# One branch per half of an expert's job, the narrow half in line, with counts and positions read later

## The chip, the cores and the metric

The kernel runs on one NeuronCore of one Trainium2 chip. Its time is the device time of one execution in microseconds (us). Five engines take part: TensorE (PE, the matrix engine), VectorE (DVE), ScalarE (ACT), GpSimd (POOL) and SyncE (SP), which here only issues DMAs. Each engine runs its own instruction stream; semaphores order them against each other, and when the program branches on a value, every engine takes the branch in its own stream.

## The reference

Three layers in float32, one after another, on 1152 tokens of width 512:

```python
attn: phi(x) = [exp(p - max|p|), exp(-(p - max|p|))], p = x @ w_phi
      out = phi(q) @ (phi(k)^T v) / (phi(q) @ sum(phi(k)) + 1e-6)       # 2 x 8 heads, 576 tokens, 64 wide
moe:  expert_idx = argmax(x @ w_gate); each expert keeps its first 288 tokens
      y = relu(x_e @ w1[e]) @ w2[e]; out[token] = gate * y               # 8 experts, F = 1024
moe2: P = exp(logits - max), 8 rounds of row and column normalisation
      out = sum over e of P[:, e] * (relu(x @ w1[e]) @ w2[e])            # 8 experts, all tokens
```

## The kernel before

Every float32 product is made of three matmuls: each operand is split into a high part (H) and a rest (L), and H*H, L*H and H*L are added up in PSUM (`three`, lines 198 to 200). The high part of a weight tile is a copy on ACT (`split`, L155), the rest a subtraction on DVE or POOL (L158). The same pair for data that leave PSUM is L193 on ACT and L194 on DVE (`split2`).

The attention fills the first 143 us of the span. The first mixture layer (149 to 336 us) is eight jobs, one for each expert. A job is wide if its expert has more than 128 tokens: the 288 token columns are the moving operand (`job_wide`). Otherwise it is narrow, with 128 tokens (`job_narrow`). With these inputs jobs 0, 1 and 4 are wide and 2, 3, 5, 6 and 7 narrow. Which one runs is decided on the chip: `tc.If(counts[j] > P)` holds the wide job, `Else` the narrow one, so a narrow job jumps over the wide one, and a wide job jumps over the narrow one at its end. On PE a wide job is some 200 rows of the program and a narrow one some 110.

A job has two halves. The first multiplies the tokens x1 by the expert's w1 and keeps the ReLU as h1; the second multiplies h1 by w2 and writes the tokens' result to x2H and x2L. In the second half the next job's tokens are transposed (`win_T`, L668, into x1H and x1L) and the next expert's w1 tiles are split (w0H, w0L: the name counts from 0), and as each split ends the DMA of the tile after that is issued on SP (L144 for w1 in two pieces of 256 KB, L147 for w2). A narrow job transposes its hidden result with `turn_h` (L721), makes its second product in two pieces of 256 columns, evicts them as yn0 and yn1 (L749), transposes these (L759) and splits the result into x2H and x2L.

PSUM tiles come from a ring of five banks, pb0 to pb4, counted by `ring["n"]` while the program is written. The two branches of a job start from one value of the counter; after both the wide job's value stands. When a bank is used again, its first writer waits for the last reader of the use before. Before the first job stand the reads of the counts and of `kept_r` into registers on every engine, the first tokens' transposes, 12 copies each that zero x2H (POOL) and x2L (DVE), and `positions()` (12 small operations on DVE and nine scatters to `tk` on POOL), with the load of `tokc` on SP.

The second mixture layer (336 us to the end) takes a fast branch: 32 units, all but the first of seven products each (`unit`, `prod` L1001), with the products by w2 of the unit before (`second`) between them. Unit 0 is plain (`first_plain`) and prepares the mixed operands (`mix`, on DVE, POOL and ACT); of its eight second products four follow it at once and four stand in unit 1. `sink_at` gives the places of the normalisation steps.

Of the kernel before, what the change touches and what calls it, by code (L numbers as in the profile page):

```python
# [13 lines left out]
AF = mybir.ActivationFunctionType  # L14
# [6 lines left out]
def kernel(  # L21
# [15 lines left out]
    nc = tc.nc  # L37
    B, H, S, D = q.shape
    N, DM = out.shape
    E, _, F = moe_w1.shape  # L40
    P = 128
# [83 lines left out]
    class Weights:  # L125
# [8 lines left out]
        def load(self, i, which, p):  # L134
            if i >= len(self.seq):
                return
            e = self.seq[i][2]
            src = self.seq[i][which]
            t = self.raw[which, p]
            if which == 0:  # L140
                a = src[e].rearrange("(c p) (h q f) -> q p c h f", p=P, h=2, f=P)[p]
                t = t.rearrange("p a (b h f) -> p (a b) h f", h=2, f=P)
                for h in range(2):
                    nc.sync.dma_start(out=t[:, :, h, :], in_=a[:, :, h, :])  # L144
            else:
                a = src[e].rearrange("(h q p) d -> q p h d", p=P, h=2)[p]
                nc.sync.dma_start(out=t, in_=a)  # L147

        def split(self, i, which, p, eng=None, copy=None):
# [493 lines left out]
    with ExitStack() as mctx:  # L643
# [32 lines left out]
        def job_wide(j, off_r):  # L676
            i, w = jobs[j]
            hint(j)
            for kk, f in enumerate(FO):
                ps = bank(W)  # L680
                for c in range(NC):
                    three(ps, wt.w1(f, c), x1[c], c, NC)
                evict_split(h1H[:, kk, :], h1L[:, kk, :], ps, relu=True)
                if i > 0 and kk < 4 and w == 0:
                    wt.split(i, 1, kk)
            pg = prep(0)
            for d in range(NC):
                ps = bank(W)
                for kk, f in enumerate(FO):
                    wH, wL = wt.w2(f)  # L690
                    three(ps, (wH[:, d * P:(d + 1) * P], wL[:, d * P:(d + 1) * P]),
                          (h1H[:, kk, :], h1L[:, kk, :]), kk, NFC)
                evict_split(x2H[:, d, ds(off_r, W)], x2L[:, d, ds(off_r, W)], ps)
                for c in ((0, 1), (2,), (3,), ())[d]:
                    win_T(j + 1, c)
                if d == 2:
                    win_load(j + 2)
                if w == NW - 1:
                    if i + 1 < E:
                        wt.split(i + 1, 0, d)  # L700
                    else:
                        next(pg)

        def job_narrow(j, off_r):
            i, w = jobs[j]
            hint(j)
            pool = {(1, 3), (0, 1), (0, 3)}

            pg = prep(0)

            def split(i, which, p):
                if i == E:
                    next(pg)
                else:
                    wt.split(i, which, p, nc.gpsimd if (which, p) in pool else None)

            def turn_h(g):
                ps = bank4()
                for f in range(4):
                    o = f % 2 * P  # L720
                    nc.tensor.transpose(ps[:, f, :], hn[2 * g + f // 2][:, o:o + P], ident)  # L721
                split2(h1H[:, 4 * g:4 * g + 4, 0:P], h1L[:, 4 * g:4 * g + 4, 0:P], ps)

            if i > 0:
                split(i, 1, 0)
            for p in range(4):
                ps = bank(256)
                for c in range(NC):
                    three(ps, (x1[c][0][:, 0:P], x1[c][1][:, 0:P]), wt.w1p(p, c), c, NC)
                nc.scalar.activation(out=hn[p], in_=ps, func=AF.Relu)  # L730
                if i > 0 and p < 3:
                    split(i, 1, p + 1)
                if p == 1:
                    ring["n"] += 1
                if p == 2:
                    turn_h(0)
            win_T(j + 1, 0)
            win_T(j + 1, 1)
            turn_h(1)
            ring["n"] += 1  # L740
            split(i + 1, 0, 0)
            split(i + 1, 0, 1)
            for g in range(2):
                ps = bank(256)
                for kk, f in enumerate(FO):
                    wH, wL = wt.w2(f)
                    n = slice(g * 256, (g + 1) * 256)
                    three(ps, (h1H[:, kk, 0:P], h1L[:, kk, 0:P]), (wH[:, n], wL[:, n]), kk, NFC)
                nc.scalar.activation(out=yn[g], in_=ps, func=AF.Copy)  # L749
                if g == 0:  # L750
                    win_T(j + 1, 2)
                    split(i + 1, 0, 2)
            win_T(j + 1, 3)
            win_load(j + 2)
            ring["n"] += 1
            ps = bank4()
            for c in range(NC):
                o = c % 2 * P
                nc.tensor.transpose(ps[:, c, :], yn[c // 2][:, o:o + P], ident)  # L759
            split(i + 1, 0, 3)  # L760
            split2(x2H[:, :, ds(off_r, P)], x2L[:, :, ds(off_r, P)], ps)
# [33 lines left out]
                src[0:1, j:j + 1], min_val=0, max_val=N, skip_runtime_bounds_check_because=why,  # L795
                **({"engines": engines} if engines else {}))

        kept_r = scalar(kept_i, 0)
        counts = [scalar(cnt_i, j) for j in range(E)] if NW == 1 else None
        for c in range(NC):  # L800
            win_T(0, c)
        win_load(1)
        for t, eng in ((x2H, nc.gpsimd), (x2L, nc.vector)):
            for c in range(NC):
                for o in range(0, N, 512):
                    n = min(512, N - o)
                    eng.tensor_copy(t[:, c, o:o + n], zero[:, 0:n])
        positions()
        nc.sync.dma_start(out=tokc, in_=tk.rearrange("(t p) o -> p t o", p=P))
        for j in range(len(jobs)):  # L810
            off_r = scalar(off_i, j, DYN)
            if NW > 1:
                job_wide(j, off_r)
                continue
            n0 = ring["n"]
            with tc.If(counts[j] > P) as cmp:
                job_wide(j, off_r)
            n1, ring["n"] = ring["n"], n0
            with cmp.Else():
                job_narrow(j, off_r)  # L820
            ring["n"] = n1

    skp = ctx.enter_context(tc.tile_pool(name="skp", bufs=1))
    gms = skp.tile([P, 96], F32, name="gms")
# [117 lines left out]
    def moe2_fast(fp):  # L942
# [88 lines left out]
                put(t)  # L1031

        pending = [sink_start, sink_max, sink_exp, sink_row] + [lambda it=it: sink_col(it) for it in range(8)]
        sink_at = ((1, 3), (1, 6), (2, 0), (2, 1), (2, 3), (2, 5), (2, 7), (3, 1), (3, 3), (3, 5), (3, 7), (4, 1))

        def relu_split(dst, src):
            hi, lo = dst
# [4 lines left out]
        def first_plain():  # L1042
# [5 lines left out]
            for i in range(4):  # L1048
# [12 lines left out]
                if i == 0:  # L1061
                    for c in range(NC):
                        gate2(c)
                    sink_logits()
            next(ms[1])
            next(ms[0])
            wt.load(E + 1, 0, 1)
            for t in range(4):
                second(0, t)
                if t < 2:  # L1070
                    next(ms[1])
            return [slots[4], slots[5]]

# [55 lines left out]

        spare = first_plain()  # L1130
        for g in range(1, 4 * E):
            spare = unit(g, spare, list(range(4 if g == 1 else 0, 8)))
        for t in range(8):
            second(4 * E - 1, t)

# [37 lines left out]
```

## Time and profile before

| what | value |
|---|---|
| median of 3 runs | 1014.09 us (1012.7 to 1018.23) |
| profiled execution | 1013.54 us, its span 1011.8 us |
| attention / first layer / second layer, from the first matmul of each | to 149.13 / 149.13 to 336.01 / 336.01 to 1011.8 us |
| PE busy | 960.1 us, 95% of the span |
| mean granted TensorE clock | 0.98 |
| starts of jobs 0 to 7 on PE | 149.13, 180.19, 211.59, 233.72, 249.43, 281.91, 297.77, 319.15 us |

PE is nearly always busy in the second layer; its idle time lies in the first 370 us, above all between jobs. So the page's shares say little, and the timeline around each job says most: a row there is a start, a duration, the engine, the line, the operation with its tiles, and in brackets the idle time of the engine ahead of it with what ended it. "issue" means that the profile shows nothing that the engine waited for.

### The profile page before, as it was taken

How to read it: one execution, taken by the hardware profiler on the slowest of the kernel's cores; microseconds unless marked ns; L12 is line 12 of the kernel's file. 1: busy time of each engine (PE TensorE's matmuls, PEld its weight loads, DVE VectorE, ACT ScalarE, POOL GpSimd, SP SyncE). 2: the span in 40 equal slices, each digit the busy share in tenths (PEclk: the TensorE clock that was granted, in tenths of full speed). 3: DMA queues.
4: the chain of work that ended last, by engine and by line, in shares of the span. 5: the costliest groups of instructions: out<-in, count | busy, mean ns of one | idle time of the engine just before them, and what ended most of it. 6: DMA issues, size and time to landing. Idle time of an engine off the chain costs nothing.

```text
span 1011.8 us, 14034 instructions
## 1 busy us (share of the span) xinstructions
PE 960.1 (95%) x5329; PEld 836.6 (83%) x5329; DVE 607.2 (60%) x1074; ACT 371.6 (37%) x621; POOL 415.4 (41%) x398
## 2 busy tenths in 40 slices
PE   8999969987987989999999999999999999999997
PEld 8999968977986767888888888888888888888886
DVE  4667765655554668856655565556555655565555
ACT  4456522556565343242232223222322232222320
POOL 2244234013023653554345434553355335533533
PEclk9999989988989999999999999999999999999999
DMA  7697121668778311122112211221122111200002
GB/s 124 142 276 248 62 87 28 194 195 226 208 203 240 94 50 42 53 63 63 41 43 63 63 42 42 63 63 41 42 62 64 43 42 48 76 23 1 1 1 84
DMA packets 123291, 89.66 MB, mean 89 GB/s; under 512 B 34529, under 2 KB 101345, under 8 KB 123201
## 3 DMA queue, kind: packets, MB, share of 16 engines
q1 hardware_dynamic: 120240, 83.65, 29.4%
q0 software_dynamic: 1728, 4.73, 1.2%
q8 instruction: 54, 0.88, 0.4%
q14 instruction: 37, 0.30, 0.1%
q10 hardware_dynamic: 1232, 0.10, 0.1%
HBM read 79.01 MB, written 9.45 MB: 87 GB/s over the span
## 4 chain that ended last, share of the span: by engine, by line
PE 79%; issue 8%; DVE 7%; ACT 2%; DMA 2%; POOL 2%; ACTq 0%; POOLq 0%; DVEq 0%; SPq 0%
PE pb L1001 27%; PE pb L198 14%; PE pb L199 14%; PE pb L200 14%; PE pb L310 3%; PE pb L445 3%; PE pb L428 1%; DMA raw<-in_moe_w_dram 1%; PE pb L668 1%; DVE hidL L1039 1%; POOL out_dram L177 1%; DVE snap L978 1%; PE pb L254 1%; DMA wg<-in_moe_w_gate_dram 1%; DVE w1L L158 0%
## 5 line engine op out<-in xcount | busy, mean ns | idle before, releaser
L1029 DVE SCALAR_TENSOR_TENSOR oc<-pb,Pm,oc 128x512 f32<-128x512 f32 x224 | 167.2, 749 | 93.8 <-PE pb L200 92.7
L955 POOL TENSOR_TENSOR w1L<-raw,w1H 128x1024 fp32r<-128x1024 f32 x32 | 77.0, 2408 | 336.1 <-ACT w1H L954 336.1
L198 PE MATMUL pb<-w1H,hidH 128*128 128x512 f32 x512 | 199.7, 390 | 3.8 <-ACT oc L1023 2.3
L200 PE MATMUL pb<-w1H,hidL 128*128 128x512 f32 x512 | 199.3, 389 | 0.0
L199 PE MATMUL pb<-w1L,hidH 128*128 128x512 f32 x512 | 199.3, 389 | 0.0
L1038 ACT ACTIVATE hidH<-snap 128x512 fp32r<-128x512 f32 x93 | 58.8, 632 | 241.6 <-DVE snap L1116 112.1
L1001 PE MATMUL pb<-x2H,w0H 128*128 128x512 f32 x310 | 121.6, 392 | 0.0
L1001 PE MATMUL pb<-x2L,w0H 128*128 128x512 f32 x310 | 120.7, 389 | 0.0
L1001 PE MATMUL pb<-x2H,w0L 128*128 128x512 f32 x310 | 120.6, 389 | 0.0
L198 PEld LDWEIGHTS pb<-w1H,hidH 128*128 128x128 f32 x512 | 96.2, 188 | 24.7 <-ACT oc L1023 2.8
L200 PEld LDWEIGHTS pb<-w1H,hidL 128*128 128x128 f32 x512 | 96.2, 188 | 20.0
L199 PEld LDWEIGHTS pb<-w1L,hidH 128*128 128x128 f32 x512 | 96.2, 188 | 20.0
L1039 DVE SCALAR_TENSOR_TENSOR hidL<-snap,hidH 128x512 fp32r<-128x512 f32 x93 | 64.6, 695 | 64.9 <-ACT hidH L1038 64.9
L640 POOL TENSOR_TENSOR w0L<-stmp,w0H 128x1024 fp32r<-128x1024 f32 x31 | 75.1, 2422 | 0.3 <-ACT w0H L637 0.3
L1001 PEld LDWEIGHTS pb<-x2H,w0L 128*128 128x128 f32 x310 | 58.2, 188 | 12.2
L1001 PEld LDWEIGHTS pb<-x2H,w0H 128*128 128x128 f32 x310 | 58.2, 188 | 11.9
L1001 PEld LDWEIGHTS pb<-x2L,w0H 128*128 128x128 f32 x310 | 58.2, 188 | 11.8
L158 POOL TENSOR_TENSOR w1L<-raw,w1H 128x1024 fp32r<-128x1024 f32 x9 | 21.7, 2409 | 109.6 <-ACT w1H L155 109.2
L635 POOL TENSOR_TENSOR w0L<-raw,w0H 128x512 fp32r<-128x512 f32 x64 | 65.3, 1044 | 0.2 <-ACT w0H L624 0.2
L1038 ACT ACTIVATE hidH<-pb 128x512 fp32r<-128x512 f32 x35 | 20.9, 596 | 88.9 <-PE pb L1001 88.9
L1001 PE MATMUL pb<-w1H,w0H 128*128 128x512 f32 x124 | 48.8, 394 | 0.0
L1001 PE MATMUL pb<-w1L,w0H 128*128 128x512 f32 x124 | 48.7, 393 | 0.0
(246 smaller groups left out, 1967.0 us busy)
## 6 DMA issues: line engine op xcount, KB each, us to landing
raw<-in_moe_w_dram SPq DMA_DIRECT2D x128, 256.0 KB, 3.6
raw<-in_moe_w_dram SPq DMA_DIRECT2D x64, 512.0 KB, 3.9
xe<-zero SPq DMA_DIRECT2D x18, 256.0 KB, 4.1
xw<-xe SPq DMA_DIRECT2D x7, 576.0 KB, 7.5
v<-in_v_dram SPq DMA_DIRECT2D x8, 256.0 KB, 5.0
q<-in_q_dram SPq DMA_DIRECT2D x8, 256.0 KB, 5.7
k<-in_k_dram SPq DMA_DIRECT2D x7, 256.0 KB, 4.8
xw<-xe SPq DMA_DIRECT2D x4, 144.0 KB, 2.7
```

What stands on the lines that cost most here:

```text
L198: nc.tensor.matmul(ps, lhsT=aH, rhs=bH, start=i == 0, stop=False)
L199: nc.tensor.matmul(ps, lhsT=aH, rhs=bL, start=False, stop=False)
L200: nc.tensor.matmul(ps, lhsT=aL, rhs=bH, start=False, stop=i == n - 1)
L310: nc.tensor.matmul(kvps[b][g // 4][:, g % 4, 0:MW], lhsT=kp[:, h, half, :], rhs=vv[:, h * VW:h * VW + MW], start=first and g % 4 == 0, sto ...
L445: nc.tensor.matmul(ps[:, h, 0:MW], lhsT=qt[:, g, :], rhs=kv[b][:, g * KW:g * KW + MW], start=half == 0, stop=half == 1,)
L635: tt(out=aL[:, o, :], in0=w, in1=aH[:, o, :].bitcast(F32), op=ALU.subtract)
L640: tt(out=sL, in0=wide(tmp), in1=sH.bitcast(F32), op=ALU.subtract)
L955: nc.gpsimd.tensor_tensor(out=lo, in0=r, in1=hi.bitcast(F32), op=ALU.subtract)
L1001: nc.tensor.matmul(o, lhsT=a[x][:, c, :], rhs=b[c][y], start=first and c == 0 and m == 0, stop=c == 1 and m == 2, skip_group_check=True)
L1029: nc.vector.scalar_tensor_tensor(out=o, in0=ps, scalar=gate, in1=o, op0=ALU.mult, op1=ALU.add)
L1038: nc.scalar.activation(out=hi, in_=src, func=AF.Relu)
L1039: nc.vector.scalar_tensor_tensor(out=lo, in0=src, scalar=0.0, in1=hi.bitcast(F32), op0=ALU.max, op1=ALU.subtract)
```

## The change

It has five parts.

1. Each job becomes two `tc.If`, one for each half, through generators with a `yield` between the halves. The test is turned round: the narrow half stands in line, and the wide half is the `Else`. All ring counts go on from the wide half, as before.
2. In a narrow job the second product is one of 512 columns in one bank. Its two evictions stand together behind it, and the split of w0 tile 2, which stood between the two pieces, stands behind them.
3. The counts are read behind the first transposes; `kept_r`, `positions()` and the load of `tokc` are put ahead of job 1; x2L is zeroed on POOL.
4. A w1 tile is loaded by one DMA of 512 KB with 1 KB pieces in place of two DMAs with 512 B pieces, by another assignment of the hidden columns to tiles; w2 follows that order.
5. In the second layer all eight `second(0, t)` stand ahead of unit 1; the stages of the operand mix stand between the last of them, and the normalisation steps get other places.

```diff
-                a = src[e].rearrange("(c p) (h q f) -> q p c h f", p=P, h=2, f=P)[p]
-                t = t.rearrange("p a (b h f) -> p (a b) h f", h=2, f=P)
-                for h in range(2):
-                    nc.sync.dma_start(out=t[:, :, h, :], in_=a[:, :, h, :])
+                a = src[e].rearrange("(c p) (q n) -> q p c n", p=P, n=2 * P)[p]
+                nc.sync.dma_start(out=t.rearrange("p a (b n) -> p (a b) n", n=2 * P), in_=a)
...
-                a = src[e].rearrange("(h q p) d -> q p h d", p=P, h=2)[p]
+                a = src[e].rearrange("(q h p) d -> q p h d", p=P, h=2)[p]
...
+            yield
             pg = prep(0)
...
+            yield
             win_T(j + 1, 0)
             win_T(j + 1, 1)
             turn_h(1)
...
+            ps = bank(512)
+            for kk, f in enumerate(FO):
+                three(ps, (h1H[:, kk, 0:P], h1L[:, kk, 0:P]), wt.w2(f), kk, NFC)
+                if kk == 3:
+                    win_T(j + 1, 2)
             for g in range(2):
-                ps = bank(256)
-                for kk, f in enumerate(FO):
-                    wH, wL = wt.w2(f)
-                    n = slice(g * 256, (g + 1) * 256)
-                    three(ps, (h1H[:, kk, 0:P], h1L[:, kk, 0:P]), (wH[:, n], wL[:, n]), kk, NFC)
-                nc.scalar.activation(out=yn[g], in_=ps, func=AF.Copy)
-                if g == 0:
-                    win_T(j + 1, 2)
-                    split(i + 1, 0, 2)
+                nc.scalar.activation(out=yn[g], in_=ps[:, g * 256:(g + 1) * 256], func=AF.Copy)
+            split(i + 1, 0, 2)
             win_T(j + 1, 3)
...
-        kept_r = scalar(kept_i, 0)
-        counts = [scalar(cnt_i, j) for j in range(E)] if NW == 1 else None
         for c in range(NC):
             win_T(0, c)
         win_load(1)
-        for t, eng in ((x2H, nc.gpsimd), (x2L, nc.vector)):
+        counts = [scalar(cnt_i, j) for j in range(E)] if NW == 1 else None
+        for t, eng in ((x2H, nc.gpsimd), (x2L, nc.gpsimd)):
...
-        positions()
-        nc.sync.dma_start(out=tokc, in_=tk.rearrange("(t p) o -> p t o", p=P))
         for j in range(len(jobs)):
+            if j == 1:
+                positions()
+                nc.sync.dma_start(out=tokc, in_=tk.rearrange("(t p) o -> p t o", p=P))
+                kept_r = scalar(kept_i, 0)
             off_r = scalar(off_i, j, DYN)
...
-            n0 = ring["n"]
-            with tc.If(counts[j] > P) as cmp:
-                job_wide(j, off_r)
-            n1, ring["n"] = ring["n"], n0
-            with cmp.Else():
-                job_narrow(j, off_r)
-            ring["n"] = n1
+            narrow_job = job_narrow(j, off_r)
+            for _ in range(2):
+                n0 = ring["n"]
+                with tc.If(counts[j] < P + 1) as cmp:
+                    next(narrow_job, None)
+                ring["n"] = n0
+                with cmp.Else():
+                    next(wide_job, None)
...
-            next(ms[1])
-            next(ms[0])
             wt.load(E + 1, 0, 1)
-            for t in range(4):
+            for t in range(8):
                 second(0, t)
-                if t < 2:
+                if t == 4:
+                    next(ms[0])
+                if t >= 4 and t < 7:
                     next(ms[1])
...
-            spare = unit(g, spare, list(range(4 if g == 1 else 0, 8)))
+            spare = unit(g, spare, list(range(8 if g == 1 else 0, 8)))
```

On PE, before, this is the end of narrow job 2 and the start of the wide version of job 3, which the narrow job 3 jumps over. The names with a number are tiles; pb3_129 is a PSUM bank.

```order
L668 MATMUL pb1_127<-ident_72,xw_1881 128x96 x3
L759 MATMUL pb3_129<-ident_72,yn0_1896 128x128 [waits Activation_49]
L759 MATMUL pb3_129<-ident_72,yn0_1896 128x128
L759 MATMUL pb3_129<-ident_72,yn1_1897 128x128 [waits Activation_49]
L759 MATMUL pb3_129<-ident_72,yn1_1897 128x128
L816 UNCONDITIONAL_BRANCH
L816 COMPARE_AND_BRANCH
L198 MATMUL pb4_130<-x1H0_1882,w0H0_142 128x288 [waits DVE_49,Activation_49]
```

The last transposes go to bank pb3, and job 3 begins in pb4. Now the same end of job 2, and behind it, on PE, the start of narrow job 3 (some 100 rows of the wide half lie between the two fences):

```order
L666 MATMUL pb2_128<-ident_72,xw_1873 128x96 x3
L757 MATMUL pb4_130<-ident_72,yn0_1888 128x128 [waits Activation_49]
L757 MATMUL pb4_130<-ident_72,yn0_1888 128x128
L757 MATMUL pb4_130<-ident_72,yn1_1889 128x128 [waits Activation_49]
L757 MATMUL pb4_130<-ident_72,yn1_1889 128x128
L819 UNCONDITIONAL_BRANCH
```

```order
L819 UNCONDITIONAL_BRANCH
L819 COMPARE_AND_BRANCH
L196 MATMUL pb4_130<-w0H0_142,x1H0_1874 128x256 [waits DVE_49,Activation_49]
L197 MATMUL pb4_130<-w0L0_143,x1H0_1874 128x256
L198 MATMUL pb4_130<-w0H0_142,x1L0_1875 128x256
```

The last transposes of job 2 and the first product of job 3 now share bank pb4, so the wait on DVE in the first row of job 3 is now for the reader of those transposes, the split into x2L.

On ACT, before, this is the second half of narrow job 2:

```order
L749 ACTIVATE yn0_1896<-pb3_129 128x256 [waits PE_49]
L193 ACTIVATE x1H2_1886<-pb4_130 128x288 [waits DVE_49,PE_49]
L155 ACTIVATE w0H2_146<-raw02_136 128x1024 [waits DMAHW6_49,DMAHW7_49,DMAHW5_49,Activation_49]
L749 ACTIVATE yn1_1897<-pb0_126 128x256 [waits DVE_49,PE_49]
L193 ACTIVATE x1H3_1888<-pb1_127 128x288 [waits DVE_49,PE_49]
L155 ACTIVATE w0H3_148<-raw03_137 128x1024 [waits DMAHW0_49,DMAHW1_49,Activation_49,Pool_49]
L193 ISA
L193 ACTIVATE x2H_1876<-pb3_129 128x4x128 [waits PE_49]
```

And now, on ACT in the same place:

```order
L191 ACTIVATE x1H2_1878<-pb1_127 128x288 [waits DVE_49,PE_49]
L749 ACTIVATE yn0_1888<-pb0_126 128x256 [waits PE_49]
L749 ACTIVATE yn1_1889<-pb0_126 128x256
L153 ACTIVATE w0H2_146<-raw02_136 128x1024 [waits DMAHW7_49,DMAHW0_49]
L191 ACTIVATE x1H3_1880<-pb2_128 128x288 [waits DVE_49,PE_49]
L153 ACTIVATE w0H3_148<-raw03_137 128x1024 [waits DMAHW1_49,Pool_49]
L191 ISA
L191 ACTIVATE x2H_1868<-pb4_130 128x4x128 [waits PE_49]
```

Behind the last matmul of the second product there are now two evictions, two weight copies and two splits, where there were one, one and two. (Lines of the changed file are two lower here: its L191 is L193 of before.)

## Rows read from the trace of the kernel before

**Rows 1.** The page: PE's busy time, share of the span, instructions.
```profile
PE   960.1 (95%) x5329; PEld 836.6 (83%) x5329; DVE 607.2 (60%) x1074; ACT 371.6 (37%) x621; POOL 415.4 (41%) x398
```

**Rows 2.** Waits of PE, 143 to 338 us: total us, times, longest.
```profile
PE pb L198 <- issue: 11.8, 4, 5.7
PE pb L198 <- DVE w1L L158: 9.4, 2, 4.7
...
PE pb L668 <- DMA xw<-xe: 2.3, 1, 2.3
```

**Rows 3.** Timeline, PE: the first matmuls of jobs 1, 2, 3 and 6.
```profile
180.19 0.30 PE L198 MATMUL pb<-x1H,w0H 128*128 128x288 f32 x1
...
211.59 0.55 PE L198 MATMUL pb<-w0H,x1H 128*128 128x256 f32 x1 [4.67 <-DVE w1L L158]
...
233.72 0.55 PE L198 MATMUL pb<-w0H,x1H 128*128 128x256 f32 x1 [5.53 <-issue]
...
297.77 0.36 PE L198 MATMUL pb<-w0H,x1H 128*128 128x256 f32 x1 [0.15 <-issue]
```

**Rows 4.** Stretches: busy us (count) of each engine, granted clock, DMA share, GB/s.
```profile
212.00:216.00 4.00, 4.00 (x20) 4.00 (x20) 0.04 (x1) 1.33 (x2) 0.00 (x0) 0.50 0.75 219
...
304.00:308.00 4.00, 1.74 (x18) 1.61 (x17) 1.50 (x4) 1.64 (x5) 2.42 (x1) 1.00 1.12 285
```

**Rows 5.** Timeline, PE: behind the first 36 matmuls of jobs 2, 3, 6.
```profile
218.28 0.60 PE L721 MATMUL pb<-ident,hn 128*128 128x128 f32 x4
...
239.70 0.60 PE L721 MATMUL pb<-ident,hn 128*128 128x128 f32 x4
...
302.13 0.60 PE L721 MATMUL pb<-ident,hn 128*128 128x128 f32 x4
```

**Rows 6.** Timeline, ACT and DVE: the end of narrow job 5.
```profile
296.74 0.38 ACT L749 ACTIVATE yn<-pb 128x256 f32<-128x256 f32 x1 [1.51 <-PE pb L200]
297.02 0.41 ACT L193 ACTIVATE x1H<-pb 128x288 fp32r<-128x288 f32 x1
297.31 1.06 ACT L155 ACTIVATE w0H<-raw 128x1024 fp32r<-128x1024 f32 x1
298.26 0.60 ACT L193 ACTIVATE x2H<-pb 128x512 f32 x1
...
298.89 0.69 DVE L194 TENSOR_TENSOR x2L<-pb,x2H 128x512 f32 x1 [0.97 <-ACT x2H L193]
```

**Rows 7.** Timeline, DVE: the last w0 split of wide job 1.
```profile
208.35 1.23 DVE L158 TENSOR_TENSOR w0L<-raw,w0H 128x1024 fp32r<-128x1024 f32 x1 [0.49 <-ACT w0H L155]
```

**Rows 8.** Timeline, PE and DVE: between the halves of jobs 1 and 2.
```profile
192.92 0.30 PE L198 MATMUL pb<-h1H,w1H 128*128 128x288 f32 x1
...
193.57 0.46 DVE L587 SCALAR_TENSOR_TENSOR h1L<-pb,h1H 128x288 fp32r<-128x288 f32 x1 [1.13 <-ACT h1H L586]
...
220.64 0.64 PE L721 MATMUL pb<-ident,hn 128*128 128x128 f32 x4
...
220.39 0.69 DVE L194 TENSOR_TENSOR h1L<-pb,h1H 128x512 fp32r<-128x512 f32 x1 [0.68 <-ACT h1H L193]
```

**Rows 9.** Timeline, PE: the first piece of job 5's second product, to its end.
```profile
290.45 0.36 PE L198 MATMUL pb<-w1H,h1H 128*128 128x256 f32 x1
...
293.40 0.41 PE L668 MATMUL pb<-ident,xw 96*128 96x96 f32 x3
```

**Rows 10.** The chain in order of time, behind the first tokens' load: start, us, what.
```profile
145.91 1.36 issue
```

**Rows 11.** Timeline, PE: the longest idle time inside job 0.
```profile
169.48 0.30 PE L200 MATMUL pb<-h1H,w1L 128*128 128x288 f32 x1 [0.84 <-issue]
```

**Rows 12.** PE at the second layer's opening: two of the timeline, two of the chain.
```profile
356.91 0.50 PE L198 MATMUL pb<-w1H,hidH 128*128 128x512 f32 x1 [1.49 <-DVE hidL L1039]
...
362.27 0.50 PE L198 MATMUL pb<-w1H,hidH 128*128 128x512 f32 x1 [2.34 <-ACT oc L1023]
...
364.05 2.56 PE pb L1001 x6
...
368.25 1.36 PE pb L1001 x6
```

More of the change, by code (lines that the diff above doesn't have):

```diff
@@ L807 @@
                     eng.tensor_copy(t[:, c, o:o + n], zero[:, 0:n])
-        positions()
-        nc.sync.dma_start(out=tokc, in_=tk.rearrange("(t p) o -> p t o", p=P))
         for j in range(len(jobs)):
+            if j == 1:
+                positions()
+                nc.sync.dma_start(out=tokc, in_=tk.rearrange("(t p) o -> p t o", p=P))
+                kept_r = scalar(kept_i, 0)
             off_r = scalar(off_i, j, DYN)
+            wide_job = job_wide(j, off_r)
             if NW > 1:
-                job_wide(j, off_r)
+                for _ in wide_job:
+                    pass
                 continue
-            n0 = ring["n"]
-            with tc.If(counts[j] > P) as cmp:
-                job_wide(j, off_r)
-            n1, ring["n"] = ring["n"], n0
-            with cmp.Else():
-                job_narrow(j, off_r)
-            ring["n"] = n1
+            narrow_job = job_narrow(j, off_r)
[6 more added lines that the diff above has]
+                    next(wide_job, None)
     skp = ctx.enter_context(tc.tile_pool(name="skp", bufs=1))
@@ L1033, in moe2_fast @@
         pending = [sink_start, sink_max, sink_exp, sink_row] + [lambda it=it: sink_col(it) for it in range(8)]
-        sink_at = ((1, 3), (1, 6), (2, 0), (2, 1), (2, 3), (2, 5), (2, 7), (3, 1), (3, 3), (3, 5), (3, 7), (4, 1))
+        sink_at = ((1, 3), (1, 5), (2, 1), (2, 2), (2, 4), (2, 6), (3, 0), (3, 2), (3, 4), (3, 6), (4, 0), (4, 2))
         def relu_split(dst, src):
```

## The prediction

> **What bounds the kernel now.** I read the page first: PE is busy for 960.1 of 1011.8 us [rows 1], so time is won where PE idles, or where it runs at the lower clock. The waits of PE put the idle time at the starts of the expert jobs: 11.8 and 9.4 us in front of a product's first matmul [rows 2]. Less 0.15 us at job 6 [rows 3] and about 0.4 us inside job 0, four gaps with a sum of 20.6 us are left. The timeline tells which: jobs 2, 3, 5 and 7 (4.67 and 5.53 us at two of them), all narrow, and none in front of jobs 1 and 4, which are wide [rows 3]. A narrow job is the one that jumps at its start, over some 200 rows. The gap "issue" has no releaser, and what is named at the other two, w1L, isn't read by the first product. So I take these gaps for the jump. One narrow job, number 6, paid only 0.15 us.
>
> [...] The first 36 matmuls took 6.69 us in job 2 (211.59 to 218.28), 5.97 us in job 3, and 4.36 us in job 6 without a gap [rows 3, 5]: 2.3 and 1.6 us lost. With about 1.4 us at each of the other two, an estimate from the smaller, that is 6.8 us.
>
> **The change part by part**, against the profiled 1013.54 us.
>
> The gaps. A narrow job no longer jumps at its start. A wide job now does, twice, over 36 to 54 rows of PE's program, and a narrow job jumps over 96 to 111 rows at the end of each half. Before, wide job 0 jumped over 114 rows at its end, and job 1 began at 180.19 us with no idle time [rows 3]. From this row I take all these jumps as free: −20.6 us, and −6.8 us of clock. Eight more branches at the middles of the jobs are priced by the nearest row, 0.15 us each [rows 3]: +1.2 us (0 to 3).
>
> What takes the place of the gaps. This is the term that decides. In the changed program the first product of a narrow job falls into the bank of the last transposes of the narrow job before, and the two branches have one count of semaphores, so that PE waits for the last DVE work of the old job: the split into x2L. Before, it waited for an x1L split only. Job 5 shows that it makes a difference: its x2L ended at 299.58 us [rows 6], job 6 had begun at 297.77 us [rows 3]. In the changed order two things more stand on ACT between the product's end and x2H: an eviction (pitch 0.28 us, 296.74 to 297.02) and the copy of w0 tile 2 (pitch 0.95 us, 297.31 to 298.26) [rows 6]. So x2L would end at 299.58 + 0.3 + 0.95 = 300.8 us. PE's last transposes, which ended at 297.62 us (297.77 less 0.15), come 0.3 us later, at 297.9 us. The gap is 2.9 us, with DVE's w0L split and the semaphores about 3.2 us (2.9 to 4.2, where the DVE split takes its longer form). It comes behind jobs 2, 3, 5 and 6: 4 × 3.2 = +12.8 us. The transposes wait for the longer eviction in each of the five narrow jobs: 5 × 0.3 = +1.5 us.
>
> Behind a wide job PE waits for the w0L split of tile 3, also the last on DVE. In job 1 it ended at 208.35 + 1.23 = 209.58 us [rows 7], PE at 211.59 − 4.67 = 206.92 us [rows 3]: 2.7 us, with the semaphore 2.8. Behind jobs 0, 1 and 4: 3 × 2.8 = +8.4 us. Nothing else on PE can cover it, as all matmuls stand in order behind the waiting one; ACT and DVE stall next, since the new job's evictions depend on it.
>
> The clock behind the new gaps. 3.2 us lies between 2.26 us, which left the clock, and 4.67 us, which halved it [rows 2 to 4]. The opening of the second layer, where idle times of 1.49 and 2.34 us came close together, was followed by six matmuls in 2.56 us in place of 1.36 [rows 12]. The narrow ends have a short pause at the transposes and then the gap, so I take the clock to fall behind these four, at 1.5 us, and not behind the 2.8 us of the wide ones: +6.0 us (0 to 16).
>
> Waits inside a job. PE's second half now begins only when the first half's last eviction is counted. In job 1 the second product began at 192.92 us, h1L ended at 194.03 us [rows 8]; its first matmul doesn't need h1L, so about 1.0 us is lost in each wide job. In job 2 the turn of the second hidden half began at 220.64 us, and would now stand behind the h1L that ends at 221.08 us [rows 8]: 0.4 us (0 to 0.7) in each narrow job. 3 × 1.0 + 5 × 0.4 = +5.0 us.
>
> The merged product. A piece takes 290.45 to 293.40, 2.95 us, so two take 5.90 us [rows 9]. Six matmuls of 512 columns take 1.36 us [rows 12], 24 take 5.44. Five narrow jobs save 0.46 us each: −2.3 us.
>
> The weight loads. SP's program is half as long for w1, and the pieces are twice as large. Only one wait of PE is a transfer, 2.3 us for the tokens xw [rows 2], where the DMA engines' share was 1.12 [rows 4]. I take it as gone: −2.3 us. Nothing more, since the jobs' pace is set by PE.
>
> The start. Before, the register reads ended 1.36 us after the first tokens had landed [rows 10]. Now the transposes begin at once, and eight reads stand between them and job 0. The trace shows no row for a read; nine of them take between 1.36 us and the whole idle time ahead of the transposes. An estimate of 3.4 us for eight gives +2.0 us (0 to 4). Zeroing x2L moves from DVE to POOL, which is free until then; the first split into x2 comes 15 us later, so this costs nothing.
>
> The counts' positions. Job 0 took 31.06 us from the start in my table to 180.19; job 1 took 180.19 to 206.92, 26.73 us [rows 3]. Of the 4.3 us, some 1.3 us is the clock at its start; 3 us stand beside the scatters, with idle time on PE of up to 0.84 us [rows 11]. The scatters now run beside job 1. SP is held by the load of `tokc` until they are done, but the loads queued behind it are needed only in job 2. Half of the stalls gone: −1.5 us (−3 to 0).
>
> The opening of the second layer. The 2.34 us wait goes, since the ACT copies no longer stand behind the mix; the half clock behind it goes with it, 2.56 − 1.36 = 1.2 us for six matmuls [rows 12] and 0.5 us for others. The 1.49 us stays, and unit 1, without second products between its own, waits about 1 us for DVE's mix. Sum −3.0 us (−4 to 0). The moved normalisation steps have covers of their size: 0.
>
> Sum: −20.6 − 6.8 + 1.2 + 12.8 + 1.5 + 8.4 + 6.0 + 5.0 − 2.3 − 2.3 + 2.0 − 1.5 − 3.0 = +0.4, so 1013.9 us. The median of the runs shown is 0.55 us above the profiled run; I leave it there.
>
> [...] The rows say that four of five long jumps cost 4.67 to 5.7 us and one cost 0.15 us [rows 2, 3]. [...]
>
> **The rivals.** One: the change does only what it says, as PE's waits at the job starts are already met when it gets there. Then 12.8, 8.4 and 6.0 us fall out of the sum: 1013.9 − 27.2 = 986.7 us. For it: the wait stands in the program before, too, and cost nothing at job 6 [rows 3]. Against it: the end of x2L and of w0L lies behind PE's end in rows 6 and 7, and the bank is the same.
>
> Two, slower: the clock falls at all seven job ends, and each time for as long as in job 2, 2.3 us, or as short as at the others, 1.5 us. That gives 7 × 1.5 to 7 × 2.3, 10.5 to 16 us, in place of 6.0: 1018 to 1024 us, about 1021. It decides from 11 us on. For it: after all four gaps of before the clock was low. Against it: 2.26 us left it alone [rows 4].
>
> Three: the short jumps still pay. Seven job ends at 5.2 us in place of the 21.2 us of waits, which run at the same time, is +15 us, with the clock +4.5 us: 1033 us. For it: job 6 shows that length alone doesn't decide. Against it: the free jump over 114 rows [rows 3].
>
> **How the numbers follow.** A measurement of this kernel can tell about 0.5%, 5 us, from no change. Forecast, the wait that moves in: 0.55, with 1013.9 us and a range of its own of 1005 to 1020 us; of it 0.13 faster, 0.38 the same, 0.04 slower. Rival one 0.23, faster. Rival two 0.18, of which 0.02 is the same. Rival three 0.04. So faster 0.36, same 0.40, slower 0.24. The range of 990 to 1022 us leaves out half of rival one and about a third of rivals two and three, 0.2 in all.
>
> **What would show it.** Right: at the starts of jobs 3, 4, 6 and 7 an idle time of about 3 us whose releaser is DVE's x2L, at jobs 1, 2 and 5 one of 2.8 us behind w0L; no idle time put down to issue; L198 with 24 matmuls of 512 columns in each narrow job; the wait for L1023 gone. Wrong: jobs that follow each other on PE within 1 us (rival one), a clock of 0.50 at seven starts (two), or 5 us behind a wide half's branch (three). The forecast is most easily wrong in the 3.2 us, since it rests on an order of ACT that I shifted by hand.

## The result, and the profile after

The changed kernel is slower: 1027.26 us (median of 6 runs, 1023.63 to 1032.52) beside 1015.46 us of the kernel before (6 runs), a ratio of 1.0121 of the mean times (95% interval 1.0098 to 1.0143). The profiled execution took 1028.04 us with a span of 1026.3 us, 14.5 us above the profiled execution of before. On another chip the same pair came out closer, 1.0072 (below).

The waits of PE in the changed kernel, 140 to 350 us (total us, times, longest), answer to [rows 2]:

```profile
PE pb L196 <- DVE x2L L192: 12.2, 4, 3.1
PE pb L196 <- issue: 6.6, 2, 3.5
PE pb L196 <- DVE w0L L156: 5.6, 2, 2.8
PE pb L666 <- DMA xw<-xe: 5.6, 2, 5.2
PE pb L196 <- DVE d L774: 2.9, 1, 2.9
PE pb L197 <- DVE h1L L585: 2.6, 3, 0.9
PE pb L666 <- DVE h1L L192: 1.7, 3, 0.6
PE pb L666 <- DMA raw<-in_moe_w_dram: 1.4, 1, 1.4
```

(`xw` are the next job's tokens and `raw` a weight tile, both as they are loaded.) No gap at a job's start is put down to issue any more: the two that are left are the start of job 0 and the start of the second layer. In place of the four gaps stand four waits for the split into x2L and three for the last DVE work of a wide job (at job 1 that is `d`, the first operation of `positions()`, which stands behind the w0L split there).

The timeline of PE, the first matmuls of jobs 0 to 7 and of the second layer (start, duration, operation, in brackets the idle time ahead and its releaser), answers to [rows 3]:

```profile
151.59 0.61 PE L196 MATMUL pb<-x1H,w0H 128*128 128x288 f32 x1 [3.06 <-issue]
...
183.99 0.37 PE L196 MATMUL pb<-x1H,w0H 128*128 128x288 f32 x1 [2.86 <-DVE d L774]
...
214.69 0.36 PE L196 MATMUL pb<-w0H,x1H 128*128 128x256 f32 x1 [2.80 <-DVE w0L L156]
...
233.69 0.55 PE L196 MATMUL pb<-w0H,x1H 128*128 128x256 f32 x1 [3.06 <-DVE x2L L192]
...
253.41 0.37 PE L196 MATMUL pb<-x1H,w0H 128*128 128x288 f32 x1 [3.06 <-DVE x2L L192]
...
285.66 0.55 PE L196 MATMUL pb<-w0H,x1H 128*128 128x256 f32 x1 [2.80 <-DVE w0L L156]
...
306.56 0.55 PE L196 MATMUL pb<-w0H,x1H 128*128 128x256 f32 x1 [3.06 <-DVE x2L L192]
...
327.27 0.55 PE L196 MATMUL pb<-w0H,x1H 128*128 128x256 f32 x1 [3.06 <-DVE x2L L192]
...
347.34 0.76 PE L196 MATMUL pb<-x2H,w0H 128*128 128x512 f32 x1 [3.54 <-issue]
```

Every job starts behind an idle time of 2.8 to 3.1 us, wide or narrow; job 0's is the one put down to issue. The second layer starts at 347.34 us, 11.3 us later than before, and takes 3.2 us more from there to the end.

The stretches behind job 2's, 5's, 6's and 7's start and the second layer's (busy us with counts of PE, PEld, DVE, ACT, POOL, then granted clock, DMA share, GB/s) answer to [rows 4]:

```profile
216.00:220.00 4.00, 4.00 (x36) 4.00 (x36) 1.98 (x2) 3.35 (x6) 0.00 (x0) 1.00 1.09 257
286.00:290.00 4.00, 4.00 (x20) 4.00 (x20) 0.65 (x1) 1.33 (x2) 0.00 (x0) 0.50 0.79 217
308.00:312.00 4.00, 4.00 (x20) 4.00 (x20) 1.82 (x2) 1.33 (x2) 0.00 (x0) 0.50 1.08 298
328.00:332.00 4.00, 4.00 (x21) 4.00 (x20) 1.82 (x2) 1.33 (x2) 0.36 (x1) 0.50 0.78 229
347.00:351.00 4.00, 3.66 (x9) 2.92 (x10) 3.35 (x2) 0.94 (x1) 2.98 (x2) 0.50 0.04 8
```

Job 2 kept a granted clock of 1.00 behind 2.80 us and ran its first 36 matmuls in 4.36 us; job 5, behind the same 2.80 us, ran at 0.50 and took 7.05 us (285.66 to 292.71). Jobs 6 and 7, at 0.50, took 6.87 and 6.76 us, and the second layer starts at 0.50 too, where it had 1.00 before (336 to 340 us).

### The profile page after: what moved, and what is told of

Read it like the earlier page. It is cut to its first block, busy times and chain, and to the rows that moved or that the text cites. A ratio compares the mean times of both kernels' runs of the same rounds, so it can differ in the third digit from the quotient of the medians.

```text
span 1026.3 us, 13709 instructions
## 1 busy us (share of the span) xinstructions
PE 969.1 (94%) x5209; PEld 836.7 (82%) x5209; DVE 602.3 (59%) x1062; ACT 373.1 (36%) x621; POOL 419.0 (41%) x410
## 4 chain that ended last, share of the span: by engine, by line
PE 82%; DVE 6%; issue 5%; ACT 3%; DMA 2%; POOL 1%; ACTq 0%; POOLq 0%; SPq 0%; DVEq 0%
PE pb L1003 26%; PE pb L196 15%; PE pb L197 15%; PE pb L198 15%; PE pb L308 3%; PE pb L443 3%; PE pb L426 1%; DMA raw<-in_moe_w_dram 1%; ACT w0H L153 1%; PE pb L666 1%; POOL out_dram L175 1%; DVE hidL L1041 1%; PE pb L252 1%; DVE x2L L192 1%; ACT x2H L191 0%
## 5 line engine op out<-in xcount | busy, mean ns | idle before, releaser
L1041 DVE SCALAR_TENSOR_TENSOR hidL<-snap,hidH 128x512 fp32r<-128x512 f32 x93 | 66.9, 719 | 64.9 <-ACT hidH L1040 64.9
L1003 PE MATMUL pb<-w1H,w0L 128*128 128x512 f32 x124 | 48.7, 393 | 0.0
```

The source lines that it names most:

```text
L1003: nc.tensor.matmul(o, lhsT=a[x][:, c, :], rhs=b[c][y], start=first and c == 0 and m == 0, stop=c == 1 and m == 2, skip_group_check=True)
L1041: nc.vector.scalar_tensor_tensor(out=lo, in0=src, scalar=0.0, in1=hi.bitcast(F32), op0=ALU.max, op1=ALU.subtract)
```

## The experiments

**The bank alone, taken out of the changed kernel.**

```diff
             win_T(j + 1, 3)
             win_load(j + 2)
-            ring["n"] += 1
             ps = bank4()
```

> The changed kernel with one line less: the second step of the bank counter in the narrow half, so that the last transposes of a narrow job (and the split into x2L that reads them) lie one bank away from the next job's first product. Theory (the shared bank makes PE wait for the last DVE work of every job, and the low clock follows from these waits): the seven idle times of 2.8 to 3.1 us at the job starts (20.7 us in the changed kernel) shrink to about 1.3 us behind narrow jobs (the x1L split of tokens' part 3 is then the last) and under 0.5 us behind wide ones, the clock no longer falls there (10.7 us in the changed kernel's trace), and the time is about 1003 us, against 1027 of the changed kernel and 1015 of before. Rival (the end of a job is bound by ACT and DVE, or by the loads, whatever bank is used): other waits of 2 to 3 us take their place and the time stays within 5 us of 1027.

Measured: 1008.36 us, a ratio to before of 0.9922 (0.9899 to 0.9944); the run of the hint beside it on the same chip, which kept all the waits at the job starts, had 1.0048. PE in this run: the first matmuls of jobs 1, 4 and 6, and the first transposes in the second half of job 2.

```profile
183.10 0.30 PE L196 MATMUL pb<-x1H,w0H 128*128 128x288 f32 x1
...
251.66 0.37 PE L196 MATMUL pb<-x1H,w0H 128*128 128x288 f32 x1 [0.31 <-issue]
...
295.59 0.36 PE L196 MATMUL pb<-w0H,x1H 128*128 128x256 f32 x1 [0.27 <-issue]
...
223.72 1.19 PE L666 MATMUL pb<-ident,xw 96*128 96x96 f32 x6 [5.29 <-DMA raw<-in_moe_w_dram]
```

The theory holds: one line of bookkeeping carried all seven waits, the ones behind wide jobs too. The gain is 5 us smaller than expected, and the last row shows an idle time of that size: PE now waits 5.29 us for a transfer in job 2. SP's row of the `tokc` load and the stretches around it show why:

```profile
206.41 0.37 SPq L807 DMA_DIRECT2D tokc<-tk  x1
```

```profile
190.00:196.00 6.00, 6.00 (x47) 5.95 (x45) 5.89 (x9) 4.92 (x10) 5.12 (x9) 1.00 0.02 1
196.00:202.00 6.00, 4.13 (x32) 3.71 (x30) 1.50 (x5) 0.68 (x2) 5.04 (x9) 1.00 0.07 4
202.00:208.00 6.00, 6.00 (x49) 6.00 (x48) 4.24 (x7) 3.46 (x7) 0.00 (x0) 1.00 0.07 4
208.00:214.00 6.00, 6.00 (x50) 6.00 (x49) 3.09 (x6) 3.33 (x6) 0.00 (x0) 1.00 0.99 330
```

SP stands at that load until the scatters are done (20 us by SP's waits). From 190 to 208 us the DMA engines move 1 to 4 GB/s, and then the w2 tiles of job 2 come all at once.

**The bank alone, put into the kernel before.**

```diff
             win_load(j + 2)
-            ring["n"] += 1
+            ring["n"] += 2
             ps = bank4()
```

> The kernel before with one edit: the bank counter of a narrow job takes one step more ahead of the last transposes, so that they share the bank of the next job's first product, as in the changed kernel; nothing else. Theory (the shared bank alone puts the waits into the program, behind wide jobs too, since both branches leave one count): the starts of jobs 1, 4 and 6, which had no idle time, get 2.8, about 2.2 and about 2.1 us, released by w0L3 and x2L; at jobs 2, 3, 5 and 7 the jump is as long as the wait and hides it. Sum +7 us, ratio 1.007. Rival (the waits of the changed kernel come from its new order of halves and copies, not from the bank): no idle time at jobs 1, 4 and 6, ratio 1.000.

Measured: ratio 1.0116 (1.0065 to 1.0166). PE, the first matmuls of jobs 1, 4 and 6, which had no idle time or 0.15 us in [rows 3]:

```profile
183.00 0.37 PE L198 MATMUL pb<-x1H,w0H 128*128 128x288 f32 x1 [2.86 <-DVE w0L L158]
...
253.84 0.37 PE L198 MATMUL pb<-x1H,w0H 128*128 128x288 f32 x1 [2.11 <-DVE x2L L194]
...
304.00 0.50 PE L198 MATMUL pb<-w0H,x1H 128*128 128x256 f32 x1 [2.12 <-DVE x2L L194]
```

The three waits came to within 0.1 us of what was expected, in a kernel that has none of the other edits. At jobs 2, 3, 5 and 7 the idle time is 4.76 to 5.64 us, no longer than the 4.67 to 5.71 us of the kernel before: there the jump hid the wait, as expected. So the bank alone is as bad as the whole change (1.0072 on this chip). The clock did not treat the two waits of 2.1 us alike: behind job 4's the granted clock stayed at 1.00, behind job 6's it fell to 0.51.

```profile
254.00:256.00 2.00, 2.00 (x16) 2.00 (x17) 0.00 (x0) 0.24 (x1) 0.92 (x1) 1.00 1.01 268
304.00:306.00 2.00, 2.00 (x9) 2.00 (x10) 1.84 (x1) 0.07 (x1) 1.08 (x1) 0.51 0.90 246
```

**The jump alone, taken out of the kernel before** (a branch per half, the narrow half in line; the last transposes fall one bank away from the next product):

```diff
+            yield
...
+            yield
...
+            wide_job = job_wide(j, off_r)
...
-            with tc.If(counts[j] > P) as cmp:
-                job_wide(j, off_r)
-            n1, ring["n"] = ring["n"], n0
-            with cmp.Else():
-                job_narrow(j, off_r)
-            ring["n"] = n1
+            narrow_job = job_narrow(j, off_r)
+            for _ in range(2):
+                n0 = ring["n"]
+                with tc.If(counts[j] < P + 1) as cmp:
+                    next(narrow_job, None)
+                ring["n"] = n0
+                with cmp.Else():
+                    next(wide_job, None)
```

> The kernel before with the first part of the change alone: a branch for each half, the narrow half in line; its counter leaves the last transposes one bank away from the next job's first product. Theory (the long jump was the gap): the four gaps of 20.6 us go, with the 6.8 us of low clock behind them; the waits between the halves add about 4.5 us, the start of the second layer about 3.5 us, and the loads, still with 512 B pieces, some 5 us of waits for transfers. Sum -14 us, ratio 0.986. Rival (the halves' jumps still cost, or the loads then bound the narrow jobs): gaps put down to issue or to raw, ratio 0.995 or more.

Measured: ratio 0.9921 (0.9896 to 0.9947), between the 0.986 of the theory and the 0.995 of the rival. The idle times of 4.67 to 5.7 us at the job starts are gone, which shows that the jump was the gap. More than half of the gain was given back, by PE's waits of this run, 143 to 335 us:

```profile
PE pb L199 <- DVE h1L L587: 9.0, 3, 7.3
PE pb L198 <- issue: 6.9, 4, 4.4
...
PE pb L198 <- DVE w0L L158: 3.7, 3, 1.3
PE pb L668 <- DMA xw<-xe: 3.3, 2, 1.8
```

7.3 us is one wait, in job 0: with `positions()` still beside job 0, the last h1L of its first half comes late there, and the new border between the halves makes PE wait for it. 4.4 us is the start of the second layer.

**A shorter queue at a narrow job's end** (the changed kernel, the shared bank kept):

```diff
                 if kk == 3:
                     win_T(j + 1, 2)
+                    split(i + 1, 0, 2)
...
-            split(i + 1, 0, 2)
             win_T(j + 1, 3)
```

> The changed kernel with the split of w0 tile 2 back in the middle of the merged second product, so that ACT has one copy less between the product's end and the split into x2; the shared bank stays. Theory (the idle time at a narrow job's end is the length of ACT's and DVE's queue behind the product): the four idle times shrink from 3.06 to 2.1 us, 3.8 us in sum; if the clock then stays up behind them, 5 to 8 us more: 1015 to 1023 us. Rival (the idle time is set by something else than that queue, a branch or a fetch): 3.06 us as it was and 1027.

Measured: 1018.22 us, ratio 1.0008 (0.9989 to 1.0027), against 1.0048 of the run of the hint beside it. PE, first matmuls of jobs 3, 6 and 7, and the stretches behind them:

```profile
240.68 0.36 PE L196 MATMUL pb<-w0H,x1H 128*128 128x256 f32 x1 [2.11 <-DVE x2L L192]
...
308.62 0.36 PE L196 MATMUL pb<-w0H,x1H 128*128 128x256 f32 x1 [2.11 <-DVE x2L L192]
...
326.08 0.35 PE L196 MATMUL pb<-w0H,x1H 128*128 128x256 f32 x1 [2.11 <-DVE x2L L192]
```

```profile
241.00:245.00 4.00, 4.00 (x36) 4.00 (x35) 3.05 (x2) 2.46 (x4) 0.76 (x1) 1.00 0.97 240
309.00:313.00 4.00, 4.00 (x36) 4.00 (x36) 3.02 (x2) 2.52 (x4) 0.72 (x1) 1.00 0.99 238
327.00:331.00 4.00, 4.00 (x36) 4.00 (x35) 2.84 (x3) 2.95 (x6) 0.18 (x1) 1.00 0.68 214
```

The idle time came out at 2.11 us, where the length of the queue gave 2.1, and behind it the granted clock stays at 1.00 in all four places (at job 4 from 261 to 265 us), where it was 0.50 to 0.61 over the 4 us behind 3.06 us in the changed kernel. The edit left the waits of 2.80 us at job 2 and 2.86 us at job 1 as they were. The profiled execution itself is long (span 1022.8 us): in it job 1 takes some 6 us longer than in the changed kernel's, with idle times beside the scatters as job 0 had them before.

**The hint of the second layer.** First the hint moved alone, into the second half (two `hint(j)` calls, each behind its `yield`):

> The changed kernel with the branch hint of the second layer moved from the first half of the last job into its second half, behind the branch that stands between. Theory (the branch in the middle of job 7 takes the hint's effect away, so PE fetches the second layer late: 3.54 us of idle time put down to issue, then 12 matmuls at half clock): the idle time goes back to about 1.3 us behind x2H, the clock stays, and the time falls by 4 us to about 1023. Rival (PE waits there for job 7's last split, as at the other job ends, and issue is only a label): no change, 1027.

Measured: ratio 1.0048 (1.0028 to 1.0067), idle time 3.10 us put down to issue, first 12 matmuls in 4.5 us from the first start to the last end (2.96 in the kernel before). So the expected idle time did not come. Beside the changed kernel's two profiles (3.54 and 3.59 us, twelve matmuls in 5.46 us) the layer's start is 1.4 us shorter; the rest of what this run has over the first of them lies in the clock behind the job starts (6 us for 36 matmuls where that had 7). In the changed kernel a narrow job 7 jumps twice between the hint and the branch to the second layer, over the wide half behind each of its own; here one of these jumps is left. Then, on the best version (below), the last job's branches turned round and the hint in the second half, so that PE takes no jump between hint and branch:

```diff
+                if j == len(jobs) - 1:
+                    with tc.If(counts[j] > P) as cmp:
+                        next(wide_job, None)
+                    n1, ring["n"] = ring["n"], n0
+                    with cmp.Else():
+                        next(narrow_job, None)
+                    ring["n"] = n1
+                    continue
```

> The best version with the last job's branches turned round again, wide half in line and narrow half as Else, and the second layer's hint in its second half. In all versions with the narrow half in line, PE takes 3.1 to 4.4 us from job 7 to the second layer, put down to issue, where the kernel before took 1.3 behind x2H; moving the hint alone left 3.1. Theory (a jump that PE takes between the hint and the branch takes the hint's effect away; here none is left between them): 1.3 to 1.6 us, and the first 12 matmuls of the layer at the full clock in 3.0 us in place of 4.6; 3 us in sum, ratio 0.981. Rival (the hint has no part in it, the branch to the second layer just takes 3 us from there): 3 us as before, plus what the last job's jumps over the wide halves then cost, ratio 0.984 or more.

PE, the second layer's first matmul and job 7's, in this run:

```profile
326.56 0.47 PE L196 MATMUL pb<-x2H,w0H 128*128 128x512 f32 x1 [0.78 <-ACT x2H L191]
...
310.17 0.39 PE L196 MATMUL pb<-w0H,x1H 128*128 128x256 f32 x1 [3.50 <-issue]
```

Measured: ratio 0.9948 (0.9928 to 0.9967), worse than 0.987 without the edit. The idle time did what the theory said, 0.78 us with the wait for x2H back as its releaser. The clock did not: the first 12 matmuls took 5.02 us, where 3.0 was expected, for the granted clock fell to 0.50 behind these 0.78 us too.

```profile
326.00:328.00 2.00, 1.27 (x3) 0.85 (x4) 0.69 (x1) 0.42 (x1) 0.00 (x0) 0.85 0.06 16
328.00:330.00 2.00, 2.00 (x6) 1.56 (x5) 0.47 (x1) 1.06 (x1) 0.16 (x1) 0.50 0.01 4
```

Job 7 now jumps over a wide half, and paid 3.50 us and the low clock for it (6.03 us for its first 36 matmuls), and the second layer took 2.5 us more (678.0 against 675.6 us). The granted clock over the layer's first 50 us was 0.92, against 0.97 without the edit: it fell twice more, behind waits for DVE of 2.04 us (`hidL`) and 1.64 us (`gms`), where the run without the edit kept it behind 1.47 and 1.68 us.

**The opening of the second layer as before** (the changed kernel with the last two hunks of the diff and `sink_at` undone):

> The changed kernel with the opening of the second layer as before: four second products ahead of unit 1, the mix stages and the normalisation steps in their old places. By my prediction the new opening was worth 3 us, so the time would rise to 1030. By the trace of the changed kernel it costs about 1 us (the second layer takes 678.96 us from its first matmul, 675.79 before, of which 2.1 us is the low clock at its start; a wait of 2.80 us for ACT's snap copy stands in place of 2.34 us for oc): the time falls by 1 us, within the noise. Which of the two is nearer is what the run tells.

Measured: ratio 1.0056 (1.0033 to 1.0079). Beside the changed kernel (1.0072, on another chip) that is no difference that can be told, and no loss of 3 us. In the profiles whose second layer starts at the low clock, it took 675.5 to 678.5 us from its first matmul to the end with the old opening (eight profiles) and 677.0 to 679.5 us with the new one (five).

**The changed kernel itself on a second chip:**

> The changed kernel unaltered, beside the kernel before on this chip, as the measure for the runs next to it. Two runs with small edits of it came out at 1.0048 and 1.0056 of before with the same idle times at the job starts, while the changed kernel itself had measured 1.0121 elsewhere. If that difference is the chip's (the low clock behind a gap lasts longer on some chips: 7.0 us for the first 36 matmuls there, 6.0 in those two runs), the ratio is about 1.006 here with 6.0 us; if those two edits had each won something, it is 1.012 with 7.0 us.

Measured: 1023.89 us, ratio 1.0072 (1.0043 to 1.0101). Idle times at the job starts as in the first profile (12.2, 5.6 and 2.9 us); the first 36 matmuls of jobs 3, 5, 6 and 7 took 5.8 to 6.0 us from the first start to the last end, those of the first profile 6.0, 7.2, 7.0 and 6.9.

**The best version** joins the bank, the shorter queue, the old opening, and the `tokc` load ahead of job 4:

```diff
             if j == 1:
                 positions()
-                nc.sync.dma_start(out=tokc, in_=tk.rearrange("(t p) o -> p t o", p=P))
                 kept_r = scalar(kept_i, 0)
+            if j == 4:
+                nc.sync.dma_start(out=tokc, in_=tk.rearrange("(t p) o -> p t o", p=P))
```

> The changed kernel with four edits: the bank counter with one step less in the narrow half, the split of w0 tile 2 back in the middle of the second product, the load of tokc ahead of job 4 in place of job 1 (in the run with the bank alone SP stood 20 us behind it, the w2 tiles came 20 us later, and PE then waited 5.3 us for a transfer), and the second layer's opening as before. Theory: 0.9922 of the run with the bank alone, less about 5 us of waits for transfers and 1 to 2 us of the opening: 0.985. Rival (the loads are bound by bytes and the wait only moves on): 0.991.

> The best version so far (the changed kernel with the four edits of e7) once more, as the measure for the three runs beside it: ratio to before 0.984 (0.980 to 0.988).

Measured: 1001.04 us and 0.9836 (0.9795 to 0.9876), then 1001.85 us and 0.9870 (0.9838 to 0.9902). It beats both kernels. The wait for a raw tile is gone; what is left are waits for xw, 10.3 us with the 5.2 us at the very start. Last, the counts read ahead of the first transposes:

> The best version with the counts read ahead of the first transposes again, as in the kernel before. By my prediction the later reads put about 2 us between the transposes and job 0 (3.15 us of idle time put down to issue in the trace): the idle time behind the transposes goes, job 0 starts some 2 us earlier, ratio 0.982. Rival (the reads ahead delay the transposes by as much): ratio 0.984.

Measured: 1000.04 us, 0.9847 (0.9824 to 0.9870). Job 0 starts at 148.53 us with no idle time, not at 151.57, so the reads did cost 3 us at that place; the median moved by 1.8 us, and the intervals of the ratios overlap. With the last job turned round as well:

> The best version with both edits, the last job turned round and the counts read first: by the theories of both 0.979, by the rivals of both 0.984 or more.

Measured: 0.9889 (0.9865 to 0.9913), against 0.9847 without the turned job: a loss again, about half of that in the run of the last job alone. Job 7 starts behind 4.06 us, the second layer behind 0.78 us, and its first 12 matmuls took 5.02 us as there.

## Why the prediction was wrong, step by step

The forecast was +0.4 us; the two profiled executions differ by 14.5 us. Term by term:

| step | forecast, us | measured, us |
|---|---|---|
| gaps of the jump | −20.6 | −20.6 |
| x2L waits, four | +12.8 | +12.2 |
| waits behind wide jobs, three | +8.4 | +8.5 |
| waits inside a job | +5.0 | +4.3 |
| transposes behind the evictions | +1.5 | +1.1 |
| clock behind the job starts | −6.8 + 6.0 | 10.7 − 6.8 = +3.9 |
| start of the second layer | not in the sum | +2.2 idle, +2.5 clock |
| opening of the second layer | −3.0 | +0.7 |
| merged product | −2.3 | −0.9 |
| weight loads | −2.3 | −0.9 |
| reads at the start | +2.0 | +2.5 |
| counts' positions | −1.5 | −2.2 |
| eight more branches | +1.2 | 0 |

The measured column adds up to +13.3; 1.2 us is not assigned.

**Right: what takes the place of the gaps.** The jump's gaps went, and the shared bank's waits came in their place, at the places, with the releasers and of the size that the sum had (3.06 us for 3.2, 2.8 for 2.8). That is shown from both sides, by the run without the shared bank and by the kernel before with it. Rival one is what the kernel does with one line less, with a smaller gain than its 27 us (0.9922 of before).

**Wrong: the start of the second layer, 4.7 us.** The forecast had no term for it. It looked at the jumps between jobs, but not at the hint that the kernel before gives PE for the far branch. In the changed program PE jumps twice between hint and branch, where it did not jump before; it idles 3.54 us ahead of the layer where it had 1.31, and the layer begins at a granted clock of 0.50: its first 12 matmuls took 5.25 us (347.34 to 352.59) and 2.80 before. The turned last job, with no jump between, brought the idle time to 0.78 us; moving the hint alone, with one jump left, did not. So the jumps are the cause of the idle time, as far as these two runs tell it. Whether they act through the hint or delay the branch by themselves was not tested: no run leaves the hint out, and turning the job also moves the place from which PE takes the branch. The cause of the 2.5 us of clock stays open. With 0.78 us of idle time the granted clock was 0.50 again (328 to 330 us), and with 1.57 us (the run with the bank alone in the kernel before) the first 12 matmuls took 4.39 us, counted as above, where the kernel before, with 1.31 us, took 2.80 at a granted clock of 1.00.

**Wrong in size: the clock, 4.7 us.** The forecast had the granted clock from [rows 4], 0.50 behind the 4.67 us of job 2 and 1.00 with a single idle time of 2.26 us (4.00 less 1.74). The clock was taken to fall behind the four narrow ends only, 1.5 us each. It fell there each time, but also behind one of the three 2.8 us waits (job 5), and it stayed down longer: 1.5, 1.6, 2.7, 2.5 and 2.4 us lost at jobs 3 to 7. This is the mechanism of rival two, at five of its seven places. On the second chip the low clock was shorter (5.8 to 6.0 us for 36 matmuls in place of 6.0 to 7.2) and the ratio 1.0072; that the chip makes this difference is the nearest reading, but one profile of the kernel on each chip doesn't settle it. Put on the 1014.09 us that the forecast started from, that ratio gives 1021.4 us, inside its range of 990 to 1022 us with the same steps wrong; that would have been luck. The run with the shorter queue kept the clock up behind a shorter idle time (1.00 behind 2.11 us, four times); that the idle time alone does not decide is shown by the two waits of 2.1 us behind which it stayed once (1.00) and fell once (0.51).

**Wrong: the opening, 3.7 us.** I let a wait of ACT's copy go and kept the rest. But ACT and DVE still prepare the mix; with the copies out of the way PE waits for them elsewhere. The changed kernel's trace has one wait of 2.80 us for ACT's `snap` in place of 2.34 us for `oc`:

```profile
382.76 0.50 PE L1003 MATMUL pb<-x2H,w0H 128*128 128x512 f32 x1 [2.80 <-ACT snap L1106]
```

The low clock behind `oc`, which the sum had let go with the wait, came back behind `snap`: 0.66 from 382.3 to 387.3 us. The run with the old opening was no slower. That the mix bounds this stretch is argued from these waits, not shown by a run.

**Wrong in size: the product and the loads, 1.4 us each.** In four of the five narrow jobs the merged product took 5.92 us for 6.09, to the start of what follows it, so it saved 0.17 us where the sum had 0.46: its matmuls of 512 columns came 0.236 us apart (24 in 5.42 us, first start to last, in job 7), not 0.227. The wait for xw went, but one of 1.40 us for a raw tile came, behind SP's 18.4 us of waiting at the load of `tokc`. The prediction said that the loads behind it "are needed only in job 2": that was true, and still too late for job 2. With the waits at the job starts out of the way this grew to 5.29 us.

**Nearly right:** the reads at the start, the waits between halves, and the scatters, which cost nothing beside job 1 in this profile but some 6 us in that of the shorter queue.

## What to carry to other kernels

Here two branches share one count of semaphores, and a buffer that the end of one branch and the start of the next job had in common made PE wait for the end of the whole branch, and of the other branch too (3.06 us behind narrow jobs, 2.80 and 2.86 us behind wide ones in the changed kernel); look at which buffer the first instruction behind a branch writes, since moving it by one place was worth about 1% or more here, in either kernel. When a jump is taken away, ask what it hid: with the shared bank put into the kernel before, its four long jumps hid the wait for ACT's and DVE's queue wholly (4.76 to 5.64 us of idle time with the shared bank, 4.67 to 5.71 without). And when the order of branches changes, look at the jumps that now stand between a branch hint and its branch: here two of them went with 2.2 us more of idle time, though the edit did not touch the hint.

## What the runs showed of the hardware

- Behind the four idle times of 3.06 us at the narrow jobs' ends the granted clock was 0.50 to 0.61 over the next 4 us in the changed kernel. On the second chip the first 36 matmuls of jobs 3, 6 and 7 took 6.0 us behind the same idle time, and so did those of job 7 in the runs of the hint and of the old opening (3.06 and 3.05 us), from the first start to the last end. Behind 2.80 us it did either: in the changed kernel job 2 kept 1.00 and job 5 fell to 0.50, and on the second chip the same two jobs took 4.5 and 5.8 us for their first 36 matmuls. Behind 2.1 us it stayed at 1.00 in five places (four in the run with the shorter queue, one in the kernel before with the shared bank) and fell in one, job 6 of the latter (0.51). At the second layer's start it stayed at 1.00 behind 1.31 us and fell to 0.50 behind 0.78. So in these runs the last idle time alone does not tell what the clock does.
- In these runs a jump's cost did not follow its length. In the run with the turned last job, narrow job 7 jumps over a wide half of 96 matmuls twice: the first jump cost 3.50 us, and behind the second the next transpose starts 0.12 us after the matmul ahead of it (317.78 and 317.90 us). What decides the cost of a jump is not shown.
